# Two groups of operand sums moved from GpSimd to VectorE, and part of the second layer's weight sums moved to the second half, in a linear-attention and gated-MLP kernel

## Chip, cores and metric

The kernel runs on one core of a Trainium2 chip. The metric is the device time of one execution in microseconds; the kernel before takes 2333.4 us, the median of 3 runs (2333.1 to 2339.52).

## The reference

Tokens S = 2048, width D = 1024, hidden width F = 3584, 32 heads, all in fp32. The inputs are normalised and go through two branches, whose product is added to the input.

```python
xn = _layernorm(x, axis=-1)
s = _A_ref(xn, A_wqkv, A_wo)      # linear attention: phi(q), phi(k), kv and z per head, num / den, then wo
g = _silu(_B_ref(xn, B_w1, B_w3, B_w2))   # h = silu(xn w1) * (xn w3); h w2
return x + s * g
```

## The kernel before

**Products.** Every fp32 operand is split into a high part (copied and rounded by ScalarE, L95) and the rest (subtracted by VectorE, L96), and a product of two operands takes three matmuls (mm3, L100 to L105: high by high, high by low, low by high). On top of that stands a scheme of the Strassen kind: a block of 2 x 2 products takes 7 products instead of 8, of sums of the blocks. One gemm is 7 products of 12 matmuls of 128x512 each, in the order B11, T2, T3, T1, B21, T4, B22 (the weight's operand), into four PSUM banks a, b, c, d. The weight's sums T1 to T4 are made in place on VectorE (L451). VectorE also empties the banks while the next products run: L578 reads b, L586 reads c into the tile c22, L593 reads d, then L610 and L618 read c and d again for c21 and c12. Bank c is written twice in a gemm, by T3 and by T4, so T4 must wait until L586 has read it.

**Order of the work.** The tokens are worked on in two halves (half(h), L778). The first half does its keys and queries, then 14 pairs of gate and up gemms; the second half does the same, then the attention, then the second layer (h times w2). `hidden` (L858) takes what a pair of gate and up gemms gives: silu on ScalarE (L865), the product with up on VectorE (L868, tile `sg`), and a store of it to DRAM (`h_d`, issued by GpSimd, L872). The second layer is a product of the same kind, so it needs the sums of the blocks of h: `four_sums` (L845) makes four sums of 128x256 for each of two column blocks of a pair (L851, L852, L854, L855, tile `hs`), all on GpSimd, stored by L880.

**Side jobs.** The second layer's weight w2 needs its sums too. `weight_sums(u, half)` (L893) is one job: load two pieces of 256 KB of w2 (SyncE, L901, tile `w`), four subtractions of 128x256 in place (`sums_of`, L885 to L891, on GpSimd), and a store of 512 KB to `wt_d` (SyncE, L908). u runs over 14 and half over 2, so there are 28 jobs. `go_on` (L949) loads two jobs ahead; job tiles have four buffers. The list of side jobs is emptied one step at a time: `catch_up` (L519) takes one step after each product of the gemms. In the first half, `next_work` first prepares the second half's operands (`prepare_next`), then does the weight sums. In the second half the list holds the denominators and row products of the attention, then the attention itself. The second half's operands are loaded at its start by SyncE (L814 to L816, seven tiles A and S of four loads each), and the raw weight tiles (`wk`, `wq`, `wg`, `wu`, two buffers) by L418, also on SyncE. The second layer reads `wt_d` first at 1667.0 us (L1281).

**Order within an engine.** Each engine works its own instructions in one fixed order, which is not that of the program's text: a scheduler lays the program out on a simulated time line (L1439) and takes each engine's order from there. What is put on another engine, or into another list, therefore also shifts its neighbours.

Of the kernel before, what the change touches and what calls it, by code (L numbers as in the profile page):

```python
# [22 lines left out]
def tile_linear_attention_times_swiglu(  # L23
# [10 lines left out]
    nc = tc.nc  # L34
    x, out = x[0], out[0]
# [3 lines left out]
    NF = F // P  # L39
# [77 lines left out]
    def small(name):  # L117
        return pc.tile([P, C], F32, tag="c", name=name)

    def signed(name):  # L120
        return pc.tile([P, C], F32, tag="sg", bufs=4, name=name)

    def job_tile(shape, name):
        return praw.tile(shape, F32, tag="job", bufs=4, name=name)
# [29 lines left out]
    def operand_tiles(h):  # L154
        return {n: pa.tile([P, 2, ND // 2, C], FR, tag=n, name=f"{n}_{h}") for n in AOPS}
# [364 lines left out]
    jobs = []  # L520
# [101 lines left out]
    def phi(src, dst, z=None):  # L622
        for _ in phi_steps(src, dst, z):
            pass
# [153 lines left out]
    def half(h):  # L778
        A = operand_tiles(h)

        def keys(pair, **how):
            return gemm(ops[f"k{h}_{pair}_"], A, uses[pair], **how)

        def run(g):
            for _ in g:
                pass

        def side_by_side(*gemms):
            for _ in zip_longest(*gemms):
                pass  # L790

        def queries(pair, **how):

            def use_q(n, c, src):
                j = 2 * pair + n
                pq = signed(f"pq{h}_{j}_{c}")
                phi(src, pq)
                nc.gpsimd.dma_start(out=pq_d[j // JG][2 * h + c][:, j % JG], in_=pq)  # L798

            return gemm(ops[f"q{h}_{pair}_"], A, use_q, **how)  # L800

        uses = [key_rows(h, pair) for pair in range(ND // 2)]
        if h == 0:
            early = [ops[f"k0_{pair}_"] for pair in range(ND // 2)]
            m = [keys(pair, early=True, own=pair == 0, led=pair == 0) for pair in range(ND // 2)]
            some = mybir.EngineType
            with tc.manual_schedule(engines={some.PE, some.Activation, some.DVE, some.Pool}):
                last = Opening(A, early, m).run()
            for k in early[2:]:
                k.ask()  # L810
            early[2].then = early[3].next
        else:

            for n in AOPS:  # L814
                for k in range(ND // 2):
                    nc.sync.dma_start(out=A[n][:, :, k].bitcast(F32), in_=a_d[n][:, :, k])  # L816
        if h == 0:
            with tc.issue_after(last.ins):
                for g in m:
                    run(g)  # L820
        else:
            side_by_side(keys(0, paired=True), queries(0, paired=True))
            for pair in range(1, ND // 2):
                run(keys(pair))
                run(queries(pair))
            jobs.append((all_denominators(), False))
            for _ in row_products():
                pass
        jobs.append((attention_work(), False) if h else (next_work(), True))
        if h == 0:  # L830
            for pair in range(ND // 2):
                run(queries(pair))
        for pair in range(NF // 2):
            last = h < NH - 1 and pair == NF // 2 - 1
            gemms = [gemm(ops[f"{'gu'[e]}{h}_{pair}_"], A, use, paired=last) for e, use in enumerate(hidden(h, pair))]
            if last:
                side_by_side(*gemms)
            else:
                for g in gemms:
                    run(g)  # L840
        for j, _ in jobs:
            run(j)
        jobs.clear()

    def four_sums(x1, x2, s12, s34, e=nc.gpsimd):  # L845

        a11, a21 = (x1.rearrange("p (g t s) -> p g t s", t=2, s=P)[:, :, t] for t in range(2))
        a12, a22 = (x2.rearrange("p (g t s) -> p g t s", t=2, s=P)[:, :, t] for t in range(2))
        s1, s2 = (s12.rearrange("p (n g s) -> p n g s", n=2, s=P)[:, n] for n in range(2))
        s3, s4 = (s34.rearrange("p (n g s) -> p n g s", n=2, s=P)[:, n] for n in range(2))  # L850
        e.tensor_add(out=s1, in0=a21, in1=a22)  # L851
        e.tensor_sub(out=s2, in0=s1, in1=a11)  # L852
        yield
        e.tensor_sub(out=s3, in0=a11, in1=a21)  # L854
        e.tensor_sub(out=s4, in0=a12, in1=s2)  # L855
        yield

    def hidden(h, pair):  # L858
        sg = {}
        i = [f1 > 2 * pair for f0, f1 in FB].index(True)  # L860
        k = pair - FB[i][0] // 2

        def use_gate(n, c, src):
            sg[n, c] = signed(f"sg{h}_{pair}_{n}{c}")
            nc.scalar.activation(sg[n, c], src, AF.Silu)  # L865

        def use_up(n, c, src):
            nc.vector.tensor_mul(out=sg[n, c], in0=src, in1=sg[n, c])  # L868

            src = sg[n, c].rearrange("p (g t s) -> p g t s", t=2, s=P)[:, :, 0] if n == 0 else \  # L870
                sg[n, c].rearrange("p (e s) -> p e s", s=P)
            nc.gpsimd.dma_start(out=h_d[i][2 * h + c][:, 2 * n:4 * n + 2, k], in_=src)  # L872
            if (n, c) in ((0, 1), (1, 0)):
                sums(c)

        def sums(c):
            o = [small(f"hs{h}_{pair}_{c}_{e}") for e in range(2)]
            for e, _ in enumerate(four_sums(sg[0, c], sg[1, c], *o)):
                queue = nc.gpsimd if h == 0 or pair == NF // 2 - 1 else nc.sync
                queue.dma_start(out=h_d[i][2 * h + c][:, 6 + 4 * e:10 + 4 * e, k],  # L880
                                in_=o[e].rearrange("p (e s) -> p e s", s=P))

        return use_gate, use_up

    def sums_of(b11, b12, b21, b22):  # L885

        nc.gpsimd.tensor_sub(out=b11, in0=b12, in1=b11)  # L887
        nc.gpsimd.tensor_sub(out=b12, in0=b22, in1=b12)
        yield True
        nc.gpsimd.tensor_sub(out=b22, in0=b22, in1=b11)  # L890
        nc.gpsimd.tensor_sub(out=b21, in0=b21, in1=b22)  # L891

    def weight_sums(u, half):  # L893

        cols = slice(half * 2 * P, (half + 1) * 2 * P)

        def load():
            t = job_tile([P, 4, 2 * P], f"w2_{u}_{half}")
            for e in range(2):
                f = 2 * u + e  # L900
                nc.sync.dma_start(out=t[:, 2 * e:2 * e + 2],  # L901
                                  in_=w2[f * P:(f + 1) * P, :].rearrange("p (n c) -> p n c", c=C)[:, :, cols])
            return t

        def steps(t):
            yield from sums_of(*(t[:, i] for i in range(4)))
            yield True
            nc.sync.dma_start(out=wt_d[u][:, :, cols], in_=t)  # L908
            yield True

        return Job(load, steps)

    def next_work():

        yield from go_on([prepare_next(i) for i in range(TH // 2)])
        yield from go_on([weight_sums(u, half) for u in range(NF // 2) for half in range(2)])

    hm4 = const.tile([P, P // DH], F32, name="hm4")
    nc.vector.memset(hm4, 0.0)
# [29 lines left out]
    def go_on(work, ahead=2):  # L949

        data = [j.load() for j in work[:ahead]]
        for i, j in enumerate(work):
            yield from j.steps(data[i])
            if i + ahead < len(work):
                data.append(work[i + ahead].load())
# [132 lines left out]
    def all_denominators():  # L1088
        yield from spread_z()
        yield from go_on([j for c in range(NCH) for j in denominators(c)])  # L1090

    def attention_work():
        work = [divide(m, k) for m in range(2) for k in range(ND // 2)]
        for k in range(ND // 2):
            for e, j in enumerate(merge_wo(k)):
                work += key_values(k + e * (ND // 2)) + [j]
        work += [divide(m, k) for m in range(2, S // (2 * P)) for k in range(ND // 2)]
        yield from go_on(work, 3)
# [3 lines left out]
    for h in range(NH):  # L1102
        order = [(part, pair) for part in (1, 0) for pair in range(ND // 2)]
        if h:
            order = [(part, pair) for pair in range(ND // 2) for part in (1, 0)]
        some = [Operands(wqkv, part * D + pair * 2 * P, f"{'qk'[part]}{h}_{pair}_", h == 0 and part == 1,
                         h and part == 0 and pair == 0)
                for part, pair in order]
# [174 lines left out]
    def second_weights(i, n, k):  # L1283
        if (i, n, k) not in asked:
            ask(i, n, k, small)
        return asked[i, n, k]
# [109 lines left out]
    def layer_place(n, i, k):  # L1396
# [4 lines left out]
                      lambda n, _, k, i=i: second_weights(i, n, k),  # L1401
                      lambda m, i=i: hiddens(i, m), lambda m, t, n: acc[m][:, t, n],
# [40 lines left out]
```

## Time and profile before

| | |
|---|---|
| median of 3 runs | 2333.4 us (2333.1 to 2339.52) |
| the profiled execution | 2331.29 us |
| its span, first to last instruction | 2329.5 us |
| busy: PE, VectorE (DVE), ScalarE (ACT), GpSimd (POOL) | 2290.6, 1773.4, 929.1, 681.6 us |
| DMA | 478.70 MB, mean 205 GB/s |
| weight jobs: first subtraction, last subtraction | 484.8 and 752.7 us |

PE is TensorE's matmuls, PEld its weight loads, SPq SyncE's DMA queue. In a row of a time line stand the start, the length, the engine, the line of the kernel, the operation, the tile written and the tiles read, and in brackets how long the engine had been idle and what released it. In a row of groups, xN is the number of instructions, and then come the busy time and the mean of one in ns. "L586" is line 586 of the kernel before; lines behind the change stand 1 to 6 further down in the changed kernel.

### The profile page before, as it was taken

What the parts mean: (1) busy time and instruction counts of PE and PEld (TensorE: products, weight loads), DVE (VectorE), ACT (ScalarE), POOL (GpSimd) and SP (SyncE); (2) the same over time, 40 slices, a digit from 0 to 9 for tenths busy, and PEclk for the clock granted to TensorE, in tenths of its full rate; (3) what the DMA queues carried; (4) which work ended last, traced back from release to release, by engine and by line L of the source; (5) the groups of instructions that cost most, each with busy time, mean ns of one, the idle gap of its engine ahead of it and who ended that gap; (6) DMA issues with size and microseconds to landing.
All of it is one profiled execution on the core that took longest, in us unless ns stands there. A gap on an engine that the chain in (4) does not pass through costs nothing.

```text
span 2329.5 us, 31760 instructions
## 1 busy us (share of the span) xinstructions
PE 2290.6 (98%) x10752; PEld 1873.7 (80%) x10752; DVE 1773.4 (76%) x2820; ACT 929.1 (40%) x1645; POOL 681.6 (29%) x851
## 2 busy tenths in 40 slices
PE   6999999999999999999999999999999999999998
PEld 5888888878887888777888888888887888888876
DVE  8887888798877775557867788887755666776798
ACT  6555343433232555433242433334333624242433
POOL 3220524276766121001423344342310000000033
PEclk9999999999999999999999999999999999999999
DMA  6555556576669646776756666665756555765688
GB/s 235 163 187 179 181 163 200 164 235 206 221 225 323 210 141 210 251 256 201 223 189 189 194 196 213 203 214 171 240 173 190 182 178 181 229 204 179 195 263 265
DMA packets 353699, 478.70 MB, mean 205 GB/s; under 512 B 24208, under 2 KB 262800, under 8 KB 353424
## 3 DMA queue, kind: packets, MB, share of 16 engines
q1 hardware_dynamic: 315808, 356.58, 48.5%
q0 software_dynamic: 37728, 120.09, 15.9%
q8 instruction: 84, 1.38, 0.2%
q14 instruction: 79, 0.65, 0.1%
HBM read 305.66 MB, written 174.59 MB: 206 GB/s over the span
## 4 chain that ended last, share of the span: by engine, by line
PE 59%; DVE 4%; DMA 3%; issue 1%; ACT 1%; SPq 0%; DVEq 0%; ACTq 0%
PE g L103 2%; PE g L104 2%; PE g L105 2%; PE cB L103 1%; PE dB L105 1%; PE dB L103 1%; PE cB L105 1%; PE dB L104 1%; PE cB L104 1%; PE aB L105 1%; PE aB L104 1%; PE aB L103 1%; DMA rA22B<-h_d 1%; PE bB L103 1%; PE bB L105 1%
## 5 line engine op out<-in xcount | busy, mean ns | idle before, releaser
L872 POOL DMA_DIRECT2D h_d<-sg x112 | 82.7, 739 | 265.4 <-DVE sg L868 231.6
L1191 POOL DMA_DIRECT2D u_d<-uB x32 | 17.3, 541 | 402.7 <-DVE uB L1174 369.7
L96 DVE TENSOR_TENSOR xy<-xy,xy 128x512 fp32r<-128x512 f32 x112 | 73.0, 685 | 65.1 <-ACT xy L95 65.0
L95 ACT CAST xy<-xy 128x512 fp32r<-128x512 f32 x112 | 65.0, 620 | 102.1 <-PE g L105 57.9
L104 PE MATMUL g<-xy,xy 128*128 128x512 f32 x224 | 87.7, 391 | 0.6 <-DVE xy L96 0.5
L105 PE MATMUL g<-xy,xy 128*128 128x512 f32 x224 | 87.1, 390 | 0.0
L103 PE MATMUL g<-xy,xy 128*128 128x512 f32 x224 | 82.5, 397 | 0.0
L642 POOL DMA_DIRECT2D y_d<-y x48 | 34.9, 727 | 117.1 <-ACT y L666 69.6
L1174 DVE TENSOR_TENSOR acc<-cB,acc 128x512 f32<-128x512 f32 x50 | 34.4, 687 | 41.3 <-PE cB L105 41.3
L1174 DVE TENSOR_TENSOR acc<-dB,acc 128x512 f32<-128x512 f32 x56 | 38.5, 688 | 30.1 <-PE dB L105 29.9
L854 POOL TENSOR_TENSOR hs<-sg 128x256 f32<-128x256 f32 x56 | 58.9, 1051 | 0.0
L852 POOL TENSOR_TENSOR hs<-hs,sg 128x256 f32<-128x256 f32 x56 | 58.8, 1049 | 0.1
L103 PEld LDWEIGHTS g<-xy,xy 128*128 128x128 f32 x224 | 41.8, 188 | 13.8 <-issue 3.7
L1010 POOL DMA_DIRECT2D qs_d<-qd x32 | 18.1, 565 | 117.5 <-DVE qd L1006 88.0
L1305 POOL DMA_DIRECT2D s_d<-s x32 | 17.3, 541 | 117.8 <-DVE s L1174 69.8
L104 PEld LDWEIGHTS g<-xy,xy 128*128 128x128 f32 x224 | 42.1, 188 | 10.6 <-DVE xy L96 1.5
L855 POOL TENSOR_TENSOR hs<-sg,hs 128x256 f32<-128x256 f32 x56 | 49.1, 877 | 1.4
L851 POOL TENSOR_TENSOR hs<-sg,sg 128x256 f32<-128x256 f32 x56 | 49.0, 875 | 1.2
L105 PEld LDWEIGHTS g<-xy,xy 128*128 128x128 f32 x224 | 42.1, 188 | 9.0
L798 POOL DMA_DIRECT2D pq_d<-pq x32 | 17.5, 547 | 104.5 <-DVE pq L632 104.3
L880 POOL DMA_DIRECT2D h_d<-hs x60 | 46.3, 773 | 2.7 <-POOL hs L855 2.1
L887 POOL TENSOR_TENSOR w<-w 128x256 f32<-128x256 f32 x28 | 29.3, 1048 | 51.0 <-DMA w<-in_B_w 51.0
(5325 smaller groups left out, 8274.9 us busy)
## 6 DMA issues: line engine op xcount, KB each, us to landing
h_d<-hs POOLq DMA_DIRECT2D x60, 256.0 KB, 3.4
h_d<-sg POOLq DMA_DIRECT2D x56, 256.0 KB, 3.3
w<-in_B_w SPq DMA_DIRECT2D x56, 256.0 KB
wt_d<-w SPq DMA_DIRECT2D x28, 512.0 KB
xy<-x_d SPq DMA_DIRECT2D x28, 512.0 KB
xy<-y_d SPq DMA_DIRECT2D x28, 512.0 KB
h_d<-hs SPq DMA_DIRECT2D x52, 256.0 KB
y_d<-y POOLq DMA_DIRECT2D x48, 256.0 KB, 3.3
```

The costliest lines, as they stand in the source:

```text
L95: nc.scalar.copy(out=hi, in_=src)
L96: return nc.vector.tensor_sub(out=lo, in0=src, in1=hi.bitcast(F32))
L103: nc.tensor.matmul(acc, lhsT=wh, rhs=ah, start=start, stop=False, skip_group_check=True)
L104: nc.tensor.matmul(acc, lhsT=wh, rhs=al, start=False, stop=False, skip_group_check=True)
L105: return nc.tensor.matmul(acc, lhsT=wl, rhs=ah, start=False, stop=stop, skip_group_check=True)
L851: e.tensor_add(out=s1, in0=a21, in1=a22)
L852: e.tensor_sub(out=s2, in0=s1, in1=a11)
L854: e.tensor_sub(out=s3, in0=a11, in1=a21)
L855: e.tensor_sub(out=s4, in0=a12, in1=s2)
L872: nc.gpsimd.dma_start(out=h_d[i][2 * h + c][:, 2 * n:4 * n + 2, k], in_=src)
L880: queue.dma_start(out=h_d[i][2 * h + c][:, 6 + 4 * e:10 + 4 * e, k], in_=o[e].rearrange("p (e s) -> p e s", s=P))
L1174: return V.tensor_add(out=c, in0=src, in1=c)
```

## The change

First, `four_sums` is told its engine, and in the first half (h = 0) that is VectorE; in the second it stays GpSimd. Second, the four subtractions of each weight job are on VectorE (`sums_of` keeps GpSimd for its other caller). Third, `next_work` does only the first NOW = 14 weight jobs; the other 14 go into a list entry at the start of the second half, ahead of the denominators, and so beside the second half's keys and queries. All loads and stores stay on the queues where they were.

```diff
--- before.py
+++ after.py
@@ -811,6 +811,7 @@
             early[2].then = early[3].next
         else:
 
+            jobs.append((all_weight_sums(slice(NOW, None)), True))
             for n in AOPS:
                 for k in range(ND // 2):
                     nc.sync.dma_start(out=A[n][:, :, k].bitcast(F32), in_=a_d[n][:, :, k])
@@ -842,7 +843,7 @@
             run(j)
         jobs.clear()
 
-    def four_sums(x1, x2, s12, s34, e=nc.gpsimd):
+    def four_sums(x1, x2, s12, s34, e):
 
         a11, a21 = (x1.rearrange("p (g t s) -> p g t s", t=2, s=P)[:, :, t] for t in range(2))
         a12, a22 = (x2.rearrange("p (g t s) -> p g t s", t=2, s=P)[:, :, t] for t in range(2))
@@ -875,20 +876,20 @@
 
         def sums(c):
             o = [small(f"hs{h}_{pair}_{c}_{e}") for e in range(2)]
-            for e, _ in enumerate(four_sums(sg[0, c], sg[1, c], *o)):
+            for e, _ in enumerate(four_sums(sg[0, c], sg[1, c], *o, nc.gpsimd if h else nc.vector)):
                 queue = nc.gpsimd if h == 0 or pair == NF // 2 - 1 else nc.sync
                 queue.dma_start(out=h_d[i][2 * h + c][:, 6 + 4 * e:10 + 4 * e, k],
                                 in_=o[e].rearrange("p (e s) -> p e s", s=P))
 
         return use_gate, use_up
 
-    def sums_of(b11, b12, b21, b22):
-
-        nc.gpsimd.tensor_sub(out=b11, in0=b12, in1=b11)
-        nc.gpsimd.tensor_sub(out=b12, in0=b22, in1=b12)
+    def sums_of(b11, b12, b21, b22, e=nc.gpsimd):
+
+        e.tensor_sub(out=b11, in0=b12, in1=b11)
+        e.tensor_sub(out=b12, in0=b22, in1=b12)
         yield True
-        nc.gpsimd.tensor_sub(out=b22, in0=b22, in1=b11)
-        nc.gpsimd.tensor_sub(out=b21, in0=b21, in1=b22)
+        e.tensor_sub(out=b22, in0=b22, in1=b11)
+        e.tensor_sub(out=b21, in0=b21, in1=b22)
 
     def weight_sums(u, half):
 
@@ -903,17 +904,22 @@
             return t
 
         def steps(t):
-            yield from sums_of(*(t[:, i] for i in range(4)))
+            yield from sums_of(*(t[:, i] for i in range(4)), nc.vector)
             yield True
             nc.sync.dma_start(out=wt_d[u][:, :, cols], in_=t)
             yield True
 
         return Job(load, steps)
 
+    NOW = 14
+
     def next_work():
 
         yield from go_on([prepare_next(i) for i in range(TH // 2)])
-        yield from go_on([weight_sums(u, half) for u in range(NF // 2) for half in range(2)])
+        yield from all_weight_sums(slice(0, NOW))
+
+    def all_weight_sums(some):
+        yield from go_on([weight_sums(u, half) for u in range(NF // 2) for half in range(2)][some])
 
     hm4 = const.tile([P, P // DH], F32, name="hm4")
     nc.vector.memset(hm4, 0.0)
```

The order of instructions shows what becomes of this at three places. The first is VectorE in pair 7 of the first half, around the eviction L586 of the up gemm (`c22u_7`). Names: `wg_8` is the raw gate weight of the next pair, `T2g_8` a split of it, `w_u_half` a weight job's tile. Before:

```order
L96 TENSOR_TENSOR T2g_8__4402<-wg_8__4197,T2g_8__4402 128x512
L451 TENSOR_TENSOR wg_8__4197<-wg_8__4197 128x4x128
L586 TENSOR_TENSOR c22u_7__4443<-cu_7__4411,uu_7__4386 128x512
L96 TENSOR_TENSOR T1g_8__4426<-wg_8__4197,T1g_8__4426 128x512
L593 TENSOR_TENSOR c22u_7__4443<-du_7__4412,c22u_7__4443 128x512
L96 TENSOR_TENSOR B21g_8__4445<-wg_8__4197,B21g_8__4445 128x512
L868 TENSOR_TENSOR sg_7_11_4313<-c22u_7__4443,sg_7_11_4313 128x512
L868 TENSOR_TENSOR sg_7_00_4336<-au_7__4387,sg_7_00_4336 128x512
```

After:

```order
L888 TENSOR_TENSOR w_2_0_4468<-w_2_0_4468 128x256
L96 TENSOR_TENSOR T2g_8__4402<-wg_8__4197,T2g_8__4402 128x512
L889 TENSOR_TENSOR w_2_0_4468<-w_2_0_4468 128x256
L586 TENSOR_TENSOR c22u_7__4443<-cu_7__4411,uu_7__4386 128x512
L451 TENSOR_TENSOR wg_8__4197<-wg_8__4197 128x4x128
L96 TENSOR_TENSOR T1g_8__4426<-wg_8__4197,T1g_8__4426 128x512
L593 TENSOR_TENSOR c22u_7__4443<-du_7__4412,c22u_7__4443 128x512
L888 TENSOR_TENSOR w_1_1_4405<-w_1_1_4405 128x256
L96 TENSOR_TENSOR B21g_8__4445<-wg_8__4197,B21g_8__4445 128x512
L869 TENSOR_TENSOR sg_7_11_4313<-c22u_7__4443,sg_7_11_4313 128x512
L889 TENSOR_TENSOR w_1_1_4405<-w_1_1_4405 128x256
```

Two subtractions of job `w_2_0` now stand ahead of the eviction, and the earlier job `w_1_1` behind it; each first subtraction must have its load.

The second is SyncE's queue in pair 9, with the weight jobs' loads and stores between the raw weights. Before:

```order
L418 DMA wu_9__4673<-in_B_w 128x8x256
L908 DMA wt_d_116<-w_2_1_4570 512x1x256
L901 DMA w_3_1_4719<-in_B_w 128x2x256 x2
L908 DMA wt_d_117<-w_3_0_4633 512x1x256
L901 DMA w_4_0_4782<-in_B_w 128x2x256 x2
L418 DMA wg_10__4830<-in_B_w 128x8x256
L908 DMA wt_d_117<-w_3_1_4719 512x1x256
```

After:

```order
L418 DMA wu_9__4673<-in_B_w 128x8x256
L909 DMA wt_d_116<-w_2_1_4570 512x1x256
L902 DMA w_3_1_4719<-in_B_w 128x2x256 x2
L902 DMA w_4_0_4782<-in_B_w 128x2x256 x2
L909 DMA wt_d_117<-w_3_0_4633 512x1x256
L418 DMA wg_10__4830<-in_B_w 128x8x256
L909 DMA wt_d_117<-w_3_1_4719 512x1x256
```

The loads of jobs `w_3_1` and `w_4_0` stand next to each other now; before, the store of `w_3_0` stood between them.

The third is VectorE at the step between the halves, where the last evictions of pair 13 (`c12g_13`, `c12u_13`) stand beside the first splits for the second half's keys and queries (`wk_0`, `wq_0`). Before:

```order
L96 TENSOR_TENSOR B11q_0__6264<-wq_0__6243,B11q_0__6264 128x512
L618 TENSOR_TENSOR c12g_13__6396<-dg_13__6165,ug_13__6119 128x512
L96 TENSOR_TENSOR T3k_0__6289<-wk_0__6225,T3k_0__6289 128x512
L451 TENSOR_TENSOR wq_0__6243<-wq_0__6243 128x4x128
L451 TENSOR_TENSOR wk_0__6225<-wk_0__6225 128x4x128
L451 TENSOR_TENSOR wq_0__6243<-wq_0__6243 128x4x128
L618 TENSOR_TENSOR c12u_13__6415<-du_13__6186,uu_13__6142 128x512
L868 TENSOR_TENSOR sg_13_10_6398<-c12u_13__6415,sg_13_10_6398 128x512
L96 TENSOR_TENSOR T3q_0__6310<-wq_0__6243,T3q_0__6310 128x512
L96 TENSOR_TENSOR T2k_0__6329<-wk_0__6225,T2k_0__6329 128x512
```

After:

```order
L852 TENSOR_TENSOR hs_13_1_0_6261<-sg_13_01_6239,sg_13_11_6163 128x256
L855 TENSOR_TENSOR hs_13_1_1_6262<-sg_13_01_6239 128x256
L618 TENSOR_TENSOR c12g_13__6284<-dg_13__6075,ug_13__6036 128x512
L451 TENSOR_TENSOR wk_0__6129<-wk_0__6129 128x4x128
L451 TENSOR_TENSOR wq_0__6145<-wq_0__6145 128x4x128
L891 TENSOR_TENSOR w_7_0_6371<-w_7_0_6371 128x256
L853 TENSOR_TENSOR hs_13_1_0_6261<-hs_13_1_0_6261,sg_13_01_6239 128x256
L618 TENSOR_TENSOR c12u_13__6303<-du_13__6095,uu_13__6054 128x512
L892 TENSOR_TENSOR w_7_0_6371<-w_7_0_6371 128x256
L856 TENSOR_TENSOR hs_13_1_1_6262<-sg_13_11_6163,hs_13_1_0_6261 128x256
L96 TENSOR_TENSOR T3q_0__6204<-wq_0__6145,T3q_0__6204 128x512
L96 TENSOR_TENSOR T2k_0__6222<-wk_0__6129,T2k_0__6222 128x512
```

Between the same splits and evictions there are now the subtractions of `w_7_0`, the first of the late jobs, and the last four_sums of pair 13 (`hs_13`); `T2k_0`, the first split that the second product of the keys needs, stands behind them.

## Prediction

> **What bounds the kernel now.** I read the page's head first, for the engine that is never idle.
>
> ```profile
> span 2329.5 us, 31760 instructions
> PE 2290.6 (98%) x10752; PEld 1873.7 (80%) x10752; DVE 1773.4 (76%) x2820; ACT 929.1 (40%) x1645; POOL 681.6 (29%) x851
> ```
>
> TensorE (PE) is busy 2290.6 of 2329.5 us, so all its idle time together is 38.9 us. Then I read PE's waits between 100 and 1000 us, which covers every place that the change touches (columns: who waits, for whom; us in all, times, longest).
>
> ```profile
> PE bk__6806 L103 <- ACT T2k__6622 L95: 1.3, 1, 1.3
> PE bk__6502 L105 <- DVE T2k__6329 L96: 1.1, 1, 1.1
> PE bk__6502 L103 <- ACT T2k__6329 L95: 1.1, 1, 1.1
> PE cu__4411 L103 <- DVE c22u__4443 L586: 0.9, 1, 0.9
> PE cg__4262 L103 <- DVE c22g__4294 L586: 0.7, 1, 0.7
> ```
>
> That is the whole answer: 5.1 us. Three waits belong to the step from the first half to the second (gemms `bk`), two to the place where the weight sums start (`cg`, `cu`, both held by the eviction L586 on VectorE). So nothing that the change does on other engines can save more than 5.1 us, or 0.22% of 2331; it can only cost more than that. Next I read the busy time by stretch, to see what room VectorE has for more work (columns: stretch, its length, then PE, PEld, DVE, ACT, POOL busy with instructions, granted clock, DMA share, GB/s). 230 to 480 is pairs 0 to 6 of gate and up, 480 to 760 the pairs with weight sums and the step between the halves, 760 to 900 the second half's keys and queries.
>
> ```profile
> 230.00:480.00 250.00, 249.93 (x1124) 206.32 (x1123) 210.57 (x312) 98.06 (x167) 94.42 (x116) 1.00 0.56 175
> 480.00:760.00 280.00, 276.10 (x1213) 227.03 (x1212) 229.98 (x261) 86.01 (x146) 200.68 (x233) 1.00 0.73 247
> 760.00:900.00 140.00, 138.67 (x643) 114.56 (x642) 102.45 (x186) 77.87 (x130) 26.75 (x40) 1.00 0.51 166
> ```
>
> VectorE is at 84%, 82% and 73%; the clock is 1.00 throughout, so it plays no part. The work to be moved is in POOL's column.
>
> **What is removed from GpSimd.** Five rows of the page name it.
>
> ```profile
> L854 POOL TENSOR_TENSOR hs<-sg 128x256 f32<-128x256 f32 x56 | 58.9, 1051 | 0.0
> L852 POOL TENSOR_TENSOR hs<-hs,sg 128x256 f32<-128x256 f32 x56 | 58.8, 1049 | 0.1
> L855 POOL TENSOR_TENSOR hs<-sg,hs 128x256 f32<-128x256 f32 x56 | 49.1, 877 | 1.4
> L851 POOL TENSOR_TENSOR hs<-sg,sg 128x256 f32<-128x256 f32 x56 | 49.0, 875 | 1.2
> L887 POOL TENSOR_TENSOR w<-w 128x256 f32<-128x256 f32 x28 | 29.3, 1048 | 51.0 <-DMA w<-in_B_w 51.0
> ```
>
> The four L85x rows count both halves; the first half's 28 of each, 112 in all, move. L887 is one of four subtractions of a weight job; x28 says that there are 28 jobs, so "8 of the 22" in the change's title is not this program's count: NOW = 14 leaves 14 jobs in the first half and puts 14 into the second. All 112 subtractions go to VectorE. GpSimd is on no PE wait above, so taking 0.88 to 1.05 us apiece off it saves nothing by itself.
>
> **What it adds to VectorE.** A 128x256 sum is not on VectorE in this trace. Its bounds are the 128x128 and the 128x512 of the same kind, from VectorE's groups between 1400 and 1550 us, and between 500 and 740.
>
> ```profile
> L852 DVE TENSOR_TENSOR qd<-qd 128x128 f32<-128x128 f32 x16 | 4.5, 280 | 0.0
> L451 DVE TENSOR_TENSOR wu__4673<-wu__4673 128x512 f32<-128x512 f32 x4 | 5.4, 1343 | 0.1
> L451 DVE TENSOR_TENSOR wg__4516<-wg__4516 128x512 f32<-128x512 f32 x4 | 2.8, 692 | 0.1
> ```
>
> 280 ns for 128 columns and 692 for 512 give 1.07 ns a column and some 143 ns fixed, so about 417 ns for 256. I take 0.417; the ends are 0.280 and 0.692. By stretch: 230 to 480 gets 56 four_sums, 23 us; 480 to 760 gets 56 four_sums and 56 weight subtractions, 47 us; the 14 late jobs bring 56 subtractions, 23 us, nearly all into 740 to 900.
>
> **What it takes off VectorE.** The two L451 rows above are the same operation on the same shape, and one takes twice as long. VectorE's and GpSimd's time lines at 538 us show why.
>
> ```profile
> 529.78 1.42 POOL L891 TENSOR_TENSOR w<-w 128x256 f32<-128x256 f32 x2
> 539.87 0.74 POOL L887 TENSOR_TENSOR w<-w 128x256 f32<-128x256 f32 x1 [8.68 <-DMA w<-in_B_w]
> 541.60 0.74 POOL L888 TENSOR_TENSOR w<-w 128x256 f32<-128x256 f32 x1 [0.98 <-DMA w<-in_B_w]
> 544.26 1.19 POOL L887 TENSOR_TENSOR w<-w 128x256 f32<-128x256 f32 x1
> ```
>
> ```profile
> 537.33 0.69 DVE L96 TENSOR_TENSOR T2g__4716<-wg__4516,T2g__4716 128x512 fp32r<-128x512 f32 x1
> 538.05 0.69 DVE L451 TENSOR_TENSOR wg__4516<-wg__4516 128x512 f32<-128x512 f32 x1
> 539.28 0.69 DVE L586 TENSOR_TENSOR c22u__4757<-cu__4725,uu__4700 128x512 f32<-128x512 f32 x1 [0.53 <-PE cu__4725 L105]
> 539.93 1.23 DVE L96 TENSOR_TENSOR T1g__4740<-wg__4516,T1g__4740 128x512 fp32r<-128x512 f32 x1
> 547.44 0.69 DVE L610 TENSOR_TENSOR c21u__4818<-cu__4725,uu__4700 128x512 f32<-128x512 f32 x1 [1.33 <-PE cu__4725 L105]
> ```
>
> While GpSimd waits for its load (8.68 us up to 539.87), VectorE's splits and sums take 0.69; the split that starts at 539.93, with GpSimd's subtraction under way, takes 1.23. The eviction L586, which reads one operand from PSUM, keeps 0.69. How much that costs is in the same stretches for L451 and L96 alone (DVE busy with instructions):
>
> ```profile
> 230.00:480.00 250.00, 46.27 (x50) 1.00 0.56 175
> 480.00:760.00 280.00, 63.66 (x58) 1.00 0.73 247
> ```
>
> ```profile
> 230.00:480.00 250.00, 81.10 (x109) 1.00 0.56 175
> 480.00:760.00 280.00, 100.64 (x102) 1.00 0.73 247
> ```
>
> At 0.69 each these would be 34.5, 40.0, 75.2 and 70.4 us. The excess is 11.8 + 5.9 = 17.7 us in the first stretch and 23.6 + 30.2 = 54 us in the second. With GpSimd's sums gone I take it all off. VectorE then has 210.6 - 17.7 + 23.4 = 216 of 250 us (87%), 230.0 - 54 + 47 = 223 of 280 (80%) and 102.5 + 23 = 125 of 140 (90%). At 0.280 a sum these are 83%, 75% and 84%; at 0.692 they are 93%, 91% and 101%.
>
> A rule is worth weighing here. The Trainium skill, page "SBUF — State Buffer", section "SBUF: two separate sides", says that VectorE and GpSimd share one pair of ports, held by one of them for a whole instruction, and that of VectorE's ordinary operations only those with two SBUF inputs meet GpSimd there. The trace agrees: 1.23 us against 0.69 for L96, and 0.69 for L586. If the rule did not hold and the lengthening came from DMA traffic instead, no relief would come and the second stretch would hold 230 + 47 = 277 of 280 us.
>
> **What each step does to the path.** (a) four_sums on VectorE, pairs 0 to 6: no PE wait now, 87% after; they stand behind L868 of their own tile, so they wait for nothing new. Nothing. If that cover went, each 0.417 would delay an eviction, and evictions are some 2 us ahead, as (b) shows. (b) The weight sums in pairs 7 to 10 now stand in VectorE's own order, ahead of L586, and wait there for their load. The time lines show the room: bank c is free for L586 at 539.2, and TensorE writes it again with the product that ends at 547.4 (L610 waits for it), which at 2.72 us a product (a 19.05 us gemm of seven) begins about 544.7. SyncE's time line has the loads:
>
> ```profile
> 531.78 0.37 SPq L418 DMA_DIRECT2D wu__4673<-in_B_w  x1
> 532.32 0.57 SPq L908 DMA_DIRECT2D wt_d<-w  x1
> 532.93 1.36 SPq L901 DMA_DIRECT2D w<-in_B_w  x2
> 534.40 0.96 SPq L908 DMA_DIRECT2D wt_d<-w  x1
> 535.40 1.99 SPq L901 DMA_DIRECT2D w<-in_B_w  x2
> ```
>
> The first job's load of 532.93 has landed by 541.60 at the latest, as the sub L888 shows, the second's of 535.40 by 544.26. In the new order both loads stand together ahead of the second store, so the second is issued some 1 us or more earlier and lands by about 543. VectorE meets that second job first, then L586: 543 + 0.42 + 0.42 + 0.69 is 544.5, against 544.7. So it just fits, and I cost it at nothing; the two waits of 0.7 and 0.9 at the start may go or turn into a wait of up to 2 us for the very first load. Between -1.6 and +2, I take 0. (c) The step between the halves: the late jobs' loads replace the last jobs' stores and loads ahead of the second half's operands in SyncE's queue (512 KB each, as many bytes as before), and VectorE runs one job's four subtractions (1.7 us) between the weight splits, while its L451 there get back from 1.2 and 2.3 us. About even; the ACT wait of 1.3 probably goes, since the cast of T2 stands earlier. Between -3.5 and +2, I take -1. (d) The denominators and the attention's jobs queue behind 14 weight jobs, a few steps later; the weight sums are first read at 1667 us. Nothing.
>
> The sum is 2331.3 (the profiled execution: span 2329.5 and 1.8 around it) - 1 = 2330; the median of the runs, 2333.4, lies 2.1 above the profiled one, so **2332** on the runs' scale.
>
> **Rivals.** *VectorE becomes the wait.* Its price is set by (b): if the second load lands after 543.2, every us beyond goes to TensorE, once per gemm, in the 7 gemms that 14 jobs fill. At the 544.26 of the trace of before, 1.1 us x 7 is 8 us; and since a gemm that ends late issues its next loads late, nothing catches it up. In the second half's keys and queries the same pattern, at 90% of VectorE, would add as much again: 8 to 16 us, **2340 to 2348**. For it: the spare time is a few tenths of a us, GpSimd waited 51.0 us for these loads in order, and VectorE cannot do that for free. Against: a scheduler that puts loads earlier, and 80% of VectorE in that stretch. *The gain is larger than the waits.* If L586, the split and the step between the halves all go free, 2331.3 - 5.1 + 2.1 = **2328**; more than that has no place in the profile. It is within 0.3% as well; a gain of over 7 us would need TensorE's own instructions to get shorter, which at a clock of 1.00 nothing shows. *The change does little of what it says:* GpSimd still issues the h_d stores, so the relief of 72 us may be partial; at half of it VectorE is at 90%, 89% and 90%, PE is still the bound, **2332** again, but with (b) a little later.
>
> **How the numbers follow.** A measurement of this kernel can tell about 0.3%, or 7 us. Even, 2327 to 2339: 0.58 (the likeliest, with the partial relief and the larger gain in it). VectorE becomes the wait: 0.36. Faster by over 0.3%: 0.06. The likeliest's own range is 2328 to 2337; the range of 8 in 10 takes in the rival up to 2350, and 2327 at the low end.
>
> **What would show it.** Right: VectorE's 128x256 sums near 0.42; L451 and L96 at 0.69 up to 760 us; VectorE's busy time in 480 to 760 below 230; PE's waits in 100 to 1000 us still some 5 us. Wrong by the rival: PE waits on L586 in pairs 7 to 10 of 1 us each, behind VectorE's wait for DMA w<-in_B_w. Wrong otherwise: PE waits on T2k, T3q and the like at 740 to 900, or anything that moves after 1000 us.

## The result and the profile after

The changed kernel takes 2386.7 us (median of 5 runs, 2382.5 to 2391.1) against 2333.4 us before (median of 5 as well, 2331.2 to 2339.5; two more runs than were there ahead of the prediction): a ratio of 1.022, 95% interval 1.021 to 1.024, 53 us slower. The forecast was 2332 us, range 2327 to 2350. The changed kernel's page begins:

```profile
span 2389.3 us, 31724 instructions
PE 2314.2 (97%) x10752; PEld 1888.1 (79%) x10752; DVE 1760.0 (74%) x3044; ACT 927.3 (39%) x1645; POOL 477.8 (20%) x627
```

GpSimd lost 204 us of work and VectorE is not busier than before (1760 against 1773 us). Nothing here says why the kernel is slower. PE's waits in the stretch on which the prediction was made, 100 to 1000 us, do not either: they come to 7.6 us, against 5.1 before (the first five of seven; 3.9 us of the seven lie between 480 and 760).

```profile
PE cg__4890 L103 <- DVE c22g__4922 L586: 1.8, 1, 1.8
PE cg__2665 L103 <- DVE c22g__2698 L586: 1.8, 1, 1.8
PE g L103 <- ACT gu L760: 1.4, 1, 1.4
PE cg__4576 L103 <- DVE c22g__4608 L586: 1.0, 1, 1.0
PE cg__4262 L103 <- DVE c22g__4294 L586: 0.9, 1, 0.9
```

The loss is found by comparing the start of each matmul, the n-th of one trace with the n-th of the other. At the row products (906 us before) the changed kernel is 3.9 us late, 1.9 of them since before 100 us, where nothing was changed, and at 1361 us 4.9; then, in the second half's last pairs of gate and up, it falls behind pair by pair, and where the attention's projection begins (1646.3 before, 1703.9 after) it is 57.6 us late, to stay about so until the end. So 52.7 us of the loss arise between 1361 and 1646 us. (The two profiled executions, 2391.1 and 2331.3 us, are 59.8 us apart, a little more than the medians.) PE's waits of the changed kernel between 1360 and 1660 us, the first six of eleven:

```profile
PE cu__12224 L103 <- DVE c22u__12259 L586: 4.8, 1, 4.8
PE cg__11737 L103 <- DVE c22g__11772 L586: 4.4, 1, 4.4
PE du__11895 L103 <- DVE c22u__11929 L593: 3.7, 1, 3.7
PE cg__12397 L103 <- DVE c22g__12432 L586: 3.5, 1, 3.5
PE cg__12727 L103 <- DVE c22g__12762 L586: 3.2, 1, 3.2
PE cu__12554 L103 <- DVE c22u__12589 L586: 3.1, 1, 3.1
```

They are waits for L586, the eviction named in the prediction, but in the second half, in which no sum was moved, and where no weight job is left. What held VectorE is in its own waits between 1300 and 1700 us; in the kernel before this row is not there.

```profile
DVE qd L1012 <- DMA qd<-pq_d: 61.2, 12, 8.9
```

L1012 (L1006 before) is the division of the attention: a job of `attention_work`, one of the side jobs of the second half, loads a tile `qd` of the queries and their reciprocal denominators (L1004, L1006 in the changed kernel), multiplies them, sums them and stores them. There are 32 of these jobs. VectorE's time line of the changed kernel shows one such wait and what stands behind it:

```profile
1445.79 0.69 DVE L451 TENSOR_TENSOR wg__12147<-wg__12147 128x512 f32<-128x512 f32 x1
1455.42 0.69 DVE L1012 SCALAR_TENSOR_TENSOR qd<-qd 128x512 f32<-128x512 f32 x1 [8.94 <-DMA qd<-pq_d]
1456.03 0.68 DVE L578 TENSOR_TENSOR uu__12198<-bu__12223,uu__12198 128x512 f32<-128x512 f32 x1
...
1458.64 0.68 DVE L586 TENSOR_TENSOR c22u__12259<-cu__12224,uu__12198 128x512 f32<-128x512 f32 x1
```

VectorE stands for 8.94 us at a division, with both evictions L578 and L586 queued behind it. SyncE's time line has the load it waits for:

```profile
1446.11 0.54 SPq L1004 DMA_DIRECT2D qd<-r_d  x1
1446.69 0.75 SPq L1006 DMA_DIRECT2D qd<-pq_d  x1
1447.48 0.54 SPq L1004 DMA_DIRECT2D qd<-r_d  x1
1448.06 1.22 SPq L1006 DMA_DIRECT2D qd<-pq_d  x1
```

The tile's four loads (two of r_d, two of pq_d) are issued from 1446.11 to 1448.06 and it is divided at 1455.42, 7.4 us after the last issue. Before, the same eviction of the same gemm (up, pair 8) stood behind a division that waited for nothing:

```profile
1424.02 0.68 DVE L1006 SCALAR_TENSOR_TENSOR qd<-qd 128x512 f32<-128x512 f32 x1
...
1426.43 0.68 DVE L586 TENSOR_TENSOR c22u__12278<-cu__12241,uu__12222 128x512 f32<-128x512 f32 x1
```

The order of instructions tells the rest. The tiles are named `qd_k`, k going 0 1 2 3 in each of eight groups. Their divisions stand in VectorE's order so; a mark < says that the job comes behind a later one:

```
before   0 1 2 3 0 1 2 3 0 1 2 3 0 1 2 3 0 1 2 3 0 1 2 3 0 1 2 3 0 1 2 3
changed  0 1 2 3 0 1 2 3 1 3 0< 1 3 2< 1 0< 3 2< 1 0< 3 2< 1 0< 3 2< 1 0< 3 2< 0< 2<
```

Joined with the trace (the n-th load row on SyncE, the n-th division on VectorE, each with its tile from the order), this gives the **lead** of each division: the time from its last load's issue to its start. Before, the last 24 have 24 to 35 us. After, the 12 odd ones have 4.3 to 7.9 us, and the even ones 41 to 69. The even tiles lie in their buffers undivided meanwhile: at 1448 us, three of the four job buffers hold loaded even tiles, and the odd jobs pass one by one through the fourth.

**The sum.** Busy time of the changed kernel and of the one before, between 1360 and 1650 us:

```profile
1360.00:1650.00 290.00, 255.51 (x1048) 206.30 (x1047) 205.58 (x346) 74.63 (x128) 104.95 (x127) 0.94 0.57 173
```

```profile
1360.00:1650.00 290.00, 290.00 (x1281) 240.15 (x1280) 241.10 (x398) 101.63 (x173) 120.39 (x144) 1.00 0.65 203
```

PE idles 34.5 us, which is the sum of the eleven waits. Its 1048 matmuls, at the 290.00 / 1281 = 0.226 us of before, would have taken 237.3 us, but took 255.5: 18.2 us more, at a granted clock of 0.94. Together that is 52.7 us, as much as the gemms fell behind there. (Both pages count the same 10752 matmuls, so the sum does not suffer from records that one trace lacks.)

### The profile page after: what moved, and what is told of

Its sections match the earlier page's. It is cut to its first block, busy times and chain, and to the rows that moved or that the text cites. A ratio compares the mean times of both kernels' runs of the same rounds, so it can differ in the third digit from the quotient of the medians.

```text
span 2389.3 us, 31724 instructions
## 1 busy us (share of the span) xinstructions
PE 2314.2 (97%) x10752; PEld 1888.1 (79%) x10752; DVE 1760.0 (74%) x3044; ACT 927.3 (39%) x1645; POOL 477.8 (20%) x627
## 4 chain that ended last, share of the span: by engine, by line
PE 68%; DMA 12%; DVE 8%; issue 8%; POOL 2%; SPq 1%; ACT 1%; DVEq 0%; POOLq 0%; ACTq 0%
DMA qd<-pq_d 3%; DMA w<-in_B_w 2%; PE g L103 2%; PE g L104 2%; PE g L105 2%; PE cB L103 1%; PE dB L103 1%; PE dB L105 1%; PE cB L105 1%; PE cB L104 1%; PE dB L104 1%; PE aB L104 1%; PE aB L105 1%; PE aB L103 1%; DMA qs_d<-qd 1%
## 5 line engine op out<-in xcount | busy, mean ns | idle before, releaser
L96 DVE TENSOR_TENSOR xy<-xy,xy 128x512 fp32r<-128x512 f32 x112 | 72.8, 686 | 60.3 <-ACT xy L95 60.3
L1012 DVE SCALAR_TENSOR_TENSOR qd<-qd 128x512 f32<-128x512 f32 x32 | 21.9, 685 | 61.2 <-DMA qd<-pq_d 61.2
L95 ACT CAST XS4B<-rS4B 128x384 fp32r<-128x384 f32 (+1 forms) x40 | 19.7, 493 | 59.5 <-PE cB L105 41.1
L798 POOL DMA_DIRECT2D pq_d<-pq x32 | 17.6, 549 | 101.6 <-DVE pq L632 101.3
L95 ACT CAST XA22B<-rA22B 128x384 fp32r<-128x384 f32 (+1 forms) x40 | 19.7, 493 | 45.8 <-PE aB L105 25.7
L95 ACT CAST XA11B<-rA11B 128x384 fp32r<-128x384 f32 (+1 forms) x40 | 19.7, 493 | 44.3 <-PE dB L105 26.8
L95 ACT CAST XS3B<-rS3B 128x384 fp32r<-128x384 f32 (+1 forms) x40 | 19.7, 493 | 41.9 <-PE bB L105 20.4
```

The source lines that it names most:

```text
L95: nc.scalar.copy(out=hi, in_=src)
L96: return nc.vector.tensor_sub(out=lo, in0=src, in1=hi.bitcast(F32))
L1012: nc.vector.scalar_tensor_tensor(t[:, :2], t[:, :2], 1e-6, t[:, 2:], op0=ALU.add, op1=ALU.mult)
```

## The experiments

Theory A: the late jobs shift the attention's jobs against the gemms, the divisions come out swapped, and VectorE, working in order, waits at each odd one for a load that was only just issued. Rival B: the moved sums, or the late jobs as such, cost the time. Rivals C and D come with the runs that tell them apart. Ratios are to the kernel before on the same chip, with 95% intervals.

**1. The change with the divisions in order.** Three side-job steps that do nothing (`empty_steps(n)` yields n times), ahead of the denominators, with everything else as in the change.

```diff
+            jobs.append((empty_steps(3), False))
             jobs.append((all_denominators(), False))
```

> The changed kernel with three empty side-job steps put in ahead of the denominators; all sums stay where the change put them and 14 jobs stay late. In the order of instructions the divisions of the second half (L1012) then stand in VectorE's order one behind the other again; in the changed kernel every second one stands ahead of the one before it. Theory A (the swapped divisions meet loads that were only just issued and hold the evictions behind them): the loss goes, 2333 to 2340 us, no PE wait on L586 after 1380 us. Rival B (VectorE has too much to do, or the late jobs are in the way): still 2380 to 2390 us.

Measured: 2331.4 us, ratio 0.9995 (0.9985 to 1.0005), a little below the range expected. The whole loss is gone, with every sum on VectorE and 14 jobs late. Leads 25 to 36 us; PE's waits between 1000 and 1700 us:

```profile
PE cs L103 <- DVE s L1192: 0.5, 1, 0.5
PE cg__9756 L103 <- DVE c22g__9786 L586: 0.2, 1, 0.2
```

**2. The kernel before with the divisions swapped.** The same edit, with 16 empty steps, in the kernel before.

> The kernel before with 16 empty side-job steps ahead of the denominators: no work is moved to another engine or place, but the attention's jobs meet the gemms 16 steps later, and the divisions stand in the swapped order of the changed kernel. Theory A: 2375 to 2395 us, with PE waits on L586 after 1380 us as in the changed kernel. Rival B: 2330 to 2337 us, since no sum was moved.

Measured: 2380.8 us, ratio 1.021 (1.019 to 1.022). No sum was moved and no job is late, and the loss is there, by the same waits (the first three of PE's between 1000 and 1700 us):

```profile
PE cu__12860 L103 <- DVE c22u__12895 L586: 4.7, 1, 4.7
PE cg__12043 L103 <- DVE c22g__12078 L586: 4.1, 1, 4.1
PE cu__12530 L103 <- DVE c22u__12565 L586: 3.9, 1, 3.9
```

Rival B fails in both directions.

**3. Only the late jobs.** The first two parts of the change undone.

```diff
-            for e, _ in enumerate(four_sums(sg[0, c], sg[1, c], *o, nc.gpsimd if h else nc.vector)):
+            for e, _ in enumerate(four_sums(sg[0, c], sg[1, c], *o, nc.gpsimd)):
-            yield from sums_of(*(t[:, i] for i in range(4)), nc.vector)
+            yield from sums_of(*(t[:, i] for i in range(4)))
```

> Only the third part of the change: 14 weight jobs late, all sums on GpSimd as before. The divisions are swapped. Theory A: 2375 to 2395 us. Rival B: if VectorE's added sums are the cause, 2330 to 2340 us.

Measured: 2387.4 us, ratio 1.023 (1.022 to 1.025). The third part of the change alone carries the loss.

**4. Only the engines.** NOW = 28 and no late jobs.

> Only the first two parts: four_sums of the first half and all 28 weight jobs on VectorE, all in the first half. The divisions are in order. Theory A: 2330 to 2345 us, with some PE waits on L586 at the weight jobs of the first half, about 1 us for each of 7 to 14 gemms. Rival B: 2380 us or more, since VectorE gets even more into the first half.

Measured: 2341.2 us, ratio 1.0035 (1.0023 to 1.0047). Divisions in order. Here, with 28 weight jobs on VectorE in the first half in place of 14, the prediction's own rival is seen: PE's first three waits between 100 and 1000 us are for L586 at the weight jobs, and VectorE holds it there.

```profile
PE cg__5204 L103 <- DVE c22g__5236 L586: 2.4, 1, 2.4
PE cg__4890 L103 <- DVE c22g__4922 L586: 2.2, 1, 2.2
PE cg__5832 L103 <- DVE c22g__5864 L586: 1.9, 1, 1.9
```

**5. The order put right, the steps left.** In the changed kernel each division is put behind the one before it; no step is added, so the attention's jobs meet the gemms where the change put them.

```diff
+            with ExitStack() as behind:
+                for x in latest:
+                    behind.enter_context(tc.issue_after(x.ins))
-            nc.vector.scalar_tensor_tensor(t[:, :2], t[:, :2], 1e-6, t[:, 2:], op0=ALU.add, op1=ALU.mult)
+                latest[:] = [nc.vector.scalar_tensor_tensor(t[:, :2], t[:, :2], 1e-6, t[:, 2:], op0=ALU.add, op1=ALU.mult)]
```

> The changed kernel, 14 jobs late and the attention's jobs at the same steps, but each division (L1012) is put behind the one before it, so that VectorE meets them in order. Theory A (it is the order of the divisions, and with it how long ahead of each its load is issued): 2329 to 2340 us, no PE wait on L586 after 1380 us. Rival C (the place of the attention's jobs against the gemms costs the time, whatever their order): 2375 us or more.

Measured: 2335.5 us, ratio 1.0003 (0.9995 to 1.0011). Leads 17.6 to 37 us, no wait for qd. It is the order and what it does to the leads, not the place of the jobs; rival C falls.

**6. Only the first eight swapped.** One empty step in the changed kernel.

> The changed kernel with one empty side-job step ahead of the denominators. The last 24 divisions then stand in order, and the first 8 are swapped (four of them ahead of an earlier one). Theory A: the loss is about a third, since 4 early-met divisions stand against 12 that cost 53 us: 2340 to 2355 us, with the PE waits at the first divisions, about 1100 us. Rival C: any of 2331 to 2390 us, with waits where the last 24 are.

Measured: 2345.4 us, ratio 1.0049 (1.0037 to 1.0061), 14 us above experiment 1. Four divisions have leads of 4.2 to 7.1 us; VectorE's waits between 1000 and 1700 us and PE's between 1050 and 1150:

```profile
DVE qd L1017 <- DMA qd<-pq_d: 15.6, 4, 5.8
```

```profile
PE cu__9250 L103 <- DVE c22u__9295 L586: 4.9, 1, 4.9
PE dg__9434 L103 <- DVE c22g__9468 L593: 2.0, 1, 2.0
```

That is 3.5 us for each early-met division, against 53 / 12 = 4.4 in the changed kernel.

**7. Meant to cut the lead, and did not.** In the kernel before, each of the last 24 jobs loads when its turn comes.

```diff
-        work += [divide(m, k) for m in range(2, S // (2 * P)) for k in range(ND // 2)]
         yield from go_on(work, 3)
+        for m in range(2, S // (2 * P)):
+            for k in range(ND // 2):
+                j = divide(m, k)
+                yield from j.steps(j.load())
```

> The kernel before, all sums and jobs where they were, but each of the last 24 divisions loads its own tile only when its turn comes and not three jobs ahead; the order stays 0 1 2 3. Theory A in its narrow form (the lead between load and division counts, and the swap only shortens it): each of 24 divisions has some 5 to 9 us of lead as the 12 early-met ones of the changed kernel, so 2350 to 2430 us, with VectorE waits for DMA qd<-pq_d. Rival D (the swap costs time by itself, for instance by evictions pushed back): 2330 to 2337 us.

Measured: 2333.1 us, ratio 0.9996 (0.9987 to 1.0004). It says nothing about rival D, since the scheduler still issued the loads 24 to 35 us ahead of their divisions: the code's place of a load isn't its place in the queue.

**8. Only the four_sums.** The first part of the change alone.

> Only the first part: the first half's four_sums on VectorE, all 28 weight jobs on GpSimd in the first half. The divisions are in order. Theory A: 2330 to 2337 us; GpSimd keeps half of its sums, so part of VectorE's relief is missing, and no weight job holds VectorE, so PE's waits in the first half stay near the kernel before.

Measured: 2331.8 us, ratio 0.9991 (0.9981 to 1.0002). Even.

**9. The lead cut, the order kept.** As in 7, and the tile first gets a memset of 4 columns (62 ns on VectorE), behind the division before it, so that the load cannot be issued sooner.

```diff
             t = job_tile([P, 4, 2 * P], f"qd{m}_{k}")
+            if m > 1:
+                with ExitStack() as behind:
+                    for x in latest:
+                        behind.enter_context(tc.issue_after(x.ins))
+                    nc.vector.memset(t[:, :, :1], 0.0)
...
-            nc.vector.scalar_tensor_tensor(t[:, :2], t[:, :2], 1e-6, t[:, 2:], op0=ALU.add, op1=ALU.mult)
+            latest[:] = [nc.vector.scalar_tensor_tensor(t[:, :2], t[:, :2], 1e-6, t[:, 2:], op0=ALU.add, op1=ALU.mult)]
```

> The kernel before, with the lead taken away and the order kept: each of the last 24 divisions loads its tile only after a small memset of it (4 columns, on VectorE), which stands behind the division before it. In VectorE's order 4 to 9 instructions lie between memset and division, so the load has about 4 to 8 us; the order stays 0 1 2 3. This is what the seventh kernel was meant to test and did not, since there the loads were still issued 24 to 33 us ahead. Theory A in its narrow form (a division that comes 4 to 8 us after its load's issue holds VectorE): 24 such divisions against 12 in the changed kernel, so 2360 to 2440 us, with VectorE waits for DMA qd<-pq_d and PE waits on L586. Rival D (the swap costs time by itself): 2331 to 2340 us.

Measured: 2378.6 us, ratio 1.019 (1.018 to 1.020), with the divisions in order and leads of 4.1 to 9.1 us. VectorE's first wait and PE's first between 1000 and 1700 us:

```profile
DVE qd L1012 <- DMA qd<-pq_d: 73.3, 18, 5.8
```

```profile
PE cg__12748 L103 <- DVE qd L999: 5.8, 1, 5.8
PE cg__13082 L103 <- DVE c22g__13119 L586: 5.6, 1, 5.6
```

(L999 is the memset. On VectorE's time line the eviction L586 of `cg__12748` starts at 1514.68 and the memset at 1515.31, so that both end within 0.02 us; what frees bank c is the eviction.) So a short lead makes such a loss without any swap, and rival D isn't needed. The loss does not go by the number of short leads: 18 of the 24 divisions waited, and PE's waits between 1340 and 1650 us come to 32 us, against 34.5 in the changed kernel with its 12. One thing more differs here: SyncE waits for the memsets too, and what is queued behind them on SyncE comes later. But in that stretch neither VectorE nor ScalarE waits for any other DMA than `qd`'s.

**10. A version that might beat both.** Experiment 1 with the weight jobs' subtractions back on GpSimd.

> A version that may beat both: four_sums of the first half on VectorE, 14 weight jobs late, but the weight jobs' subtractions on GpSimd as before, and three empty side-job steps so that the divisions stand in order. VectorE then never waits for a w2 load, and the waits at the step between the halves should stay away. By my reading of PE's waits there are at most 5 us to be had: 2327 to 2333 us. If it is GpSimd's two-input sums that keep VectorE late in the first half, PE waits of 1 to 2 us stay there and it is even.

Measured: 2339.3 us, ratio 1.0024 (1.0014 to 1.0034): slower, and outside the range expected. Its waits are mostly at the step between the halves, where I had expected none:

```profile
PE bk__6400 L103 <- ACT T2k__6222 L95: 3.5, 1, 3.5
PE trk L638 <- DVE pk L632: 2.8, 1, 2.8
PE bk__6400 L105 <- DVE T2k__6222 L96: 2.2, 1, 2.2
```

The weight jobs' engine is the only difference from experiment 1, where no wait on T2k remains. Which of those jobs, the early or the late ones, brings the waits back was not taken apart.

**11. Eight late jobs.** NOW = 20, the number of late jobs in the change's title.

> The changed kernel with NOW = 20, so that 8 weight jobs are late and 20 in the first half, all on VectorE. The divisions stand in order. Theory A: 2331 to 2340 us, between the version with none late (2341) and that with 14 late in order (2331). If late jobs as such cost time in the second half, in proportion to their number: some 2363 us.

Measured: 2334.6 us, ratio 1.0009 (1.0000 to 1.0018), divisions in order. Late jobs as such cost nothing that shows.

None of the versions is clear of the kernel before on the fast side.

## Why the prediction was wrong, step by step

**The step that failed is (d):** "The denominators and the attention's jobs queue behind 14 weight jobs, a few steps later; the weight sums are first read at 1667 us. Nothing." The jobs did move a few steps, and the sums' readers were no matter. But I took "later" for a shift of a sequence that stays the same. The sequence changed: every second division of the last 24 now stands ahead of the one before it, and its lead fell from some 28 us to 4 to 8. Experiments 2 and 3 make the loss without the moved sums, 1 and 5 remove it with them, and 9 makes it by the lead alone. The order could be had without a run; the prediction looked at it around the moved instructions, at three places, and not at the instructions that only stand behind them. Its first reading has the same gap: PE's waits between 100 and 1000 us, it says, cover every place that the change touches, and the loss is at 1361 to 1646 us. The list of what would show it wrong did name "anything that moves after 1000 us", which is what came.

What turns the order is the number of steps ahead of the attention's jobs. With 1, 2, 3, 4 or 8 empty steps in the kernel before, the order of instructions stays 0 1 2 3, and with 16 it is swapped; in the changed kernel 1 swaps the first eight alone, 2 swaps the other parity, 3 sets it right; with NOW = 12 it is swapped, and with 16, 18, 20, 22 it isn't. Why the scheduler's simulated time line takes the later job first at those phases stays open.

**The bound, 5.1 us,** held: no version came out faster beyond its interval.

**The price of a sum,** 0.417 us by interpolation, was right. VectorE's groups of the changed kernel between 230 and 760 us:

```profile
L852 DVE TENSOR_TENSOR hs<-sg,sg 128x256 f32<-128x256 f32 x28 | 11.8, 421 | 0.4
L853 DVE TENSOR_TENSOR hs<-hs,sg 128x256 f32<-128x256 f32 x28 | 11.6, 415 | 0.0
L888 DVE TENSOR_TENSOR w<-w 128x256 f32<-128x256 f32 x15 | 6.3, 420 | 22.6 <-DMA w<-in_B_w 22.6
```

**The relief** was more than forecast. VectorE's busy time by stretch, after:

```profile
230.00:480.00 250.00, 248.17 (x1111) 204.95 (x1110) 203.43 (x364) 99.67 (x167) 45.38 (x65) 0.99 0.55 173
480.00:760.00 280.00, 276.04 (x1212) 226.53 (x1211) 205.10 (x376) 85.24 (x145) 43.67 (x59) 1.00 0.59 195
760.00:900.00 140.00, 140.00 (x650) 115.77 (x649) 113.86 (x228) 76.72 (x128) 25.25 (x38) 1.00 0.72 237
```

VectorE has 203, 205 and 114 us where I had 216, 223 and 125. (One of the shares that I gave was off: at 0.280 us a sum the second stretch comes to 74%, not 75.) L451 and L96 of the second of these stretches take 40.92 us for 60 and 66.78 for 98, 0.68 each. There the DMA traffic fell too, from 247 to 195 GB/s, so this stretch alone does not rule out that DMA lengthened them. The first one does: at 173 GB/s, against 175 before, L451 takes 33.13 us for 49 and L96 73.31 for 109, 0.68 and 0.67 each, where they took 0.93 and 0.74. So the lengthening before was GpSimd's, and the forecast, which counted L451 and L96 alone, had it too small. The row of L586 on which the prediction rested the other half of the rule shows little: it ends at 539.97 us, and GpSimd's subtraction starts at 539.87. A better one is L593, which reads a bank too: between 480 and 760 us before, its 14 take 9.58 us, 0.68 each, where L96's 102 take 0.99 each. The rule of the Trainium skill on the shared ports ("SBUF — State Buffer", "SBUF: two separate sides") agrees with these.

**(a)** held but for one wait of 1.8 us, on `cg__2665` at 295 us, which experiment 1, with the same first half, doesn't have. **(b)** was off by 2.3 us in the direction of the rival. The L888 row shows VectorE waiting 22.6 us for w2 loads, and PE pays 3.9 us in 480 to 760, against 1.6 for L586 before. With 28 jobs in the first half, twice what the rival was priced for there, and none in the second (experiment 4), the kernel takes 2341 us, at the low end of the rival's 2340 to 2348. **(c)** was right, and more than the 1 us taken: the three waits on T2k, 3.5 us before, are gone, and no wait of PE is listed between 760 and 900. (b) and (c) about cancel, and experiment 1, the change without the swap, is at 2331.4 us, against 2332 forecast; that it comes so near is in part the luck of two terms that were off in opposite directions.

## What to carry to other kernels

On an engine that works in order, a change is not local to what it moves: list every instruction there that waits for a load, before and after, and compare the order and the lead of each, all the way to the end of the program, above all where jobs are dealt out step by step beside other work. The prefetch of three jobs protected nothing here once the consumer took them out of order; the lead from issue to use is the number to watch (here some 28 us was safe, 17.6 still was, 4 to 9 wasn't; between 9 and 17 nothing was run). And where such a swap hangs on the number of steps ahead, a chain on the consumers (experiment 5) is a cure that does not depend on that number; whether it also lasts through other edits was not run.

## What the runs showed of the hardware

Most of these waits of PE cost more than their own length. PE's time line of the changed kernel at the wait of 4.84 us, matmuls of one shape throughout:

```profile
1454.16 0.39 PE L104 MATMUL ag__12372<-A,B11g__12306 128*128 128x512 f32 x1
1459.38 0.68 PE L103 MATMUL cu__12224<-A,T4u__12262 128*128 128x512 f32 x1 [4.84 <-DVE c22u__12259 L586]
1459.86 0.63 PE L104 MATMUL cu__12224<-A,T4u__12262 128*128 128x512 f32 x1
1460.29 0.63 PE L105 MATMUL cu__12224<-A,T4u__12262 128*128 128x512 f32 x1
```

Starts are 0.43 us apart after the wait, against 0.23 ahead of it, and the granted clock says the same:

```profile
1460.00:1461.00 1.00, 1.00 (x4) 0.80 (x3) 1.00 (x2) 0.00 (x0) 0.00 (x0) 0.50 0.59 176
```

Between 1380 and 1610 us the trace's record of the clock has nine such spells, eight of 3.41 us and one of 6.83; together 34.1 us at half the clock, which is 17.1 us of the 18.2 in the sum above. The Trainium skill, "TensorE: Matmul & The Clock Gate", "Part 1: The HAM clock gate (the "warmup" mystery)", has the clock halved after an idle window of about 3.4 us and full again after as long a busy one. The trace agrees on the way back. On the way in, shorter waits did it too: after the wait of 2.4 us on `cu__12884` starts are 0.43 us apart, after that of 2.3 us on `dg__12068` they stay at 0.23.

What tells these two waits apart is not their length. Each of the nine spells begins a whole number of 3.41 us after the first, at 1384.44 us. If the stretch is cut into such windows, PE idled 2.04 us or more in each of the nine windows just ahead of a spell, and 1.80 or less in every other window at full clock. The wait on `dg__12068` is split over two windows, 0.49 and 1.80 us; that on `cu__12884` lies whole in one, 2.35 us. For each of them the rows show the window that holds the wait, or most of it, and the one behind it (PE busy comes first behind the length, the clock third from the end):

```profile
1435.64:1439.05 3.41, 1.61 (x7) 1.34 (x8) 3.38 (x10) 1.59 (x4) 1.29 (x3) 1.00 0.10 34
1439.05:1442.46 3.41, 3.41 (x17) 2.80 (x16) 3.32 (x8) 1.96 (x5) 1.51 (x2) 1.00 0.65 189
1551.70:1555.11 3.41, 1.06 (x5) 0.60 (x4) 3.41 (x9) 2.26 (x4) 0.97 (x2) 1.00 0.06 19
1555.11:1558.52 3.41, 3.41 (x9) 2.63 (x9) 3.41 (x8) 0.00 (x0) 1.00 (x2) 0.50 0.47 139
```

The traces of experiments 2, 3 and 9 agree between 1340 and 1650 us: 21 spells, each behind a window with 2.02 us of idle time or more, and none behind 1.83 or less. But 2 us is no fixed limit: at 2244 us in experiment 5, between matmuls that come with many short gaps, a spell followed a window with some 1.5 us. No run was made to test this.
